# Loading w_q first, in eight 16-row pieces, and giving the last sums ten rows of w_out instead of six

## The chip, the cores and the metric

The kernel runs on one core of one Trainium2 chip. A core has five engines that run their own instruction streams and wait for each other through semaphores: PE (TensorE, matrix products; PEld is its loading of stationary operands), DVE (VectorE), ACT (ScalarE), POOL (GpSimd) and SP (SyncE, which here only issues DMAs). Sixteen DMA engines move data between HBM and the on-chip memory SBUF, which has 128 partitions; PE writes its results to a second memory, PSUM. The metric is the device time of one execution in microseconds (us), lower is better. The kernel before takes 128.52 us, the median of three runs (128.49 to 128.59).

## The reference, cut to what matters

One decoding step: one token, one row `x` of 576 numbers, layer-normed to `xn`. Two branches read `xn`, and the result is their sum with `x`.

```python
xn = layernorm(x)
# A: attention over the last 4096 positions of a cache, 32 query heads, 16 key heads, head size 128
q  = (xn @ wq)                      # wq: 576 x 4096
s  = q . k_cache[..., -4096:, :] * 128 ** -0.5
a  = softmax(s) . v_cache[..., -4096:, :]
A  = a.reshape(4096) @ wo           # wo: 4096 x 576
# B: a gated MLP
z  = gelu(xn @ w_in)                # w_in: 576 x 4608
g  = w_sp * layernorm(z[2304:]) + b_sp
B  = (z[:2304] * g) @ w_out         # w_out: 2304 x 576
out = x + A + B
```

Everything is bfloat16 in HBM. Keys and values are 16.8 MB each, w_q and w_o 4.7 MB each, w_in 5.3 MB and w_out 2.7 MB: 51 MB are read for very little arithmetic.

## The kernel before

The 16 key heads are worked on in four blocks of four heads (`b` = 0 to 3). A block's keys are one tile `kn[b]` of 128 partitions, with 32 KB in each; its values `vn[b]` likewise. w_q is one tile `wq_t` with 36,864 bytes in each partition (nine rows of 2048 numbers). Tiles come from two pools with two buffers each, `small` (32 KB per partition) and `large` (36 KB), so a load into a pool's third tile waits until the first one's readers are done. Two narrow leftovers, `win8` and `wo28`, share a third buffer.

The order of the work is the order of the program text: nothing is rearranged, and every engine runs its own part in that order. All large loads are issued by SP, and they are listed at the top of the kernel (lines 105 to 124) in the order in which the DMA engines then work them off: keys 0 in two halves, w_q in two pieces of five and four rows, keys 1, values 0, keys 2, values 1, keys 3, w_in, values 2, values 3, w_o, w_out in four pieces. ACT issues three tiny loads before (`x_row` and the two numbers `ws2`). Eight completion counters are used in turn by these loads, ACT's three included, so a load's issue also waits for the load eight places before it.

The compute side:

- `turn(b)` (line 214, DVE): eight transposes that turn the keys of a block into the eight tiles `kt`, which have eight buffers in all.
- the query: 36 products of w_q with `xn` into `q_ps` (line 225, PE), then a copy (229), a transpose (231), four products (234) and four multiplications into `zq` (238).
- `scores(b)` (line 261, PE): 32 products of `zq` with the `kt` tiles; then maximum, exponential and transpose on DVE and ACT (264 to 287).
- `values(b)` (line 295, PE) and its small followers (300 to 306).
- `gate(z_all())`: the products with w_in (line 319) and the gate, ending in `hv`, the 18 columns that meet w_out.
- the end: w_o and the first `LATE` = 12 rows of w_out (of FR = 18) are summed into two PSUM tiles `acc` as four partial rows each (line 390). These are copied to `acc_sb` (393 on ACT, 394 on DVE), the PSUM tile `fin` is set to zero (396), and `late` (line 400) adds into `fin` the remaining rows of w_out, four products per row, and the four partial rows of `acc_sb`, eight instructions. Then the result is rounded (409) and stored (410).

The calls stand in this order: `turn(0)`, the query, `scores(0)`, `turn(1)`, `scores(1)`, `values(0)`, `turn(2)`, `scores(2)`, `values(1)`, `turn(3)`, `scores(3)`, `gate(z_all())`, `values(2)`, `values(3)`, the end.

Of the kernel before, what the change touches and what calls it, by code (L numbers as in the profile page):

```python
# [8 lines left out]
FP32 = mybir.dt.float32  # L9
# [5 lines left out]
P = 128  # L15
D = 576
# [12 lines left out]
NR = 9  # L29
# [3 lines left out]
FR = FH // P  # L33
# [3 lines left out]
ZW = P + ZPAD  # L37
SMALL = NU * DH
LARGE = WR * D
LATE = 12  # L40
OW = D // 4


# [1 line left out]
def kernel(  # L45
# [14 lines left out]
    nc = tc.nc  # L60
# [11 lines left out]
    ps_v = ctx.enter_context(tc.tile_pool(name="ps_v", bufs=1, space=PS))  # L72
# [11 lines left out]
    def unit(name, width):  # L84
        pool = small if width == SMALL else large
        return pool.tile([P, width], BF16, name=name, tag="u")

    def halves(a):
        return a.rearrange("k (s c) -> (k s) c", s=2).rearrange("(p r) c -> p (r c)", r=NR)

    def load(t, view, width, cuts):
        for a, e in zip(cuts, cuts[1:]):
            nc.sync.dma_start(t[:, (a - cuts[0]) * width:(e - cuts[0]) * width], view[:, a * width:e * width])

    def load_kv(cache, name, b, width, cuts=(0, NU)):
        t = unit(f"{name}{b}", width)
        src = cache[0, HB * b:HB * (b + 1), SK - W:SK, :].rearrange("s (j u) d -> j s (u d)", u=NU)
        for a, e in zip(cuts, cuts[1:]):
            nc.sync.dma_start(t[:, a * DH:e * DH], src[:, :, a * DH:e * DH])  # L99
        return t  # L100

    kn, vn = {}, {}
    wq_v, win_v = halves(A_wq), halves(B_w_in)
    wo_v = A_wo.rearrange("(p r) n -> p (r n)", r=WR)
    kn[0] = load_kv(A_k_cache, "k", 0, SMALL, (0, NU // 2, NU))
    wq_t = unit("wq", LARGE)
    load(wq_t, wq_v, 2048, (0, 5, NR))
    kn[1] = load_kv(A_k_cache, "k", 1, SMALL)
    vn[0] = load_kv(A_v_cache, "v", 0, LARGE)
    kn[2] = load_kv(A_k_cache, "k", 2, SMALL)  # L110
# [10 lines left out]
    wo28 = one.tile([P, FH], BF16, name="wo28", tag="side")  # L121
    load(wo28, wo_v, D, (28, WR))
    wout_t = unit("wout", LARGE)
    load(wout_t, B_w_out.rearrange("(p r) n -> p (r n)", r=FR), D, (0, LATE, 16, 17, FR))


    ident = const.tile([P, P], BF16, name="ident")
# [83 lines left out]
    def turn(b):  # L211
        for k in range(NK):
            t = ktp.tile([P, 2, 512, 2], BF16, name=f"kt{b}_{k}", tag="kt")
            nc.vector.transpose(  # L214
                t[:].rearrange("p c n e -> p (c n e)").bitcast(FP32),
                kn[b][:, UK * DH * k:UK * DH * (k + 1)].bitcast(FP32).rearrange("p (u c i) -> p c u i", c=2, i=32))
            kt[b, k] = t

    turn(0)


    q_ps = ps_s.tile([P, 512], FP32, name="q_ps", tag="s")
# [30 lines left out]
    def scores(b):  # L253
        sm = one.tile([P, 2, 512], FP32, name=f"sm{b}", tag="sm")
        mx = work.tile([P, 2], FP32, name=f"mx{b}", tag="mx")
        for kk in range(2):
            s_ps = ps_s.tile([P, 512], FP32, name=f"s{b}_{kk}", tag="s")
            for k4 in range(4):
                for ce in range(4):
                    c, e = divmod(ce, 2)  # L260
                    nc.tensor.matmul(s_ps[:], lhsT=zq[:, b, ce, ZPAD - 8 * k4:ZPAD - 8 * k4 + P],  # L261
                                     rhs=kt[b, 4 * kk + k4][:, c, :, e],
                                     start=k4 == 0 and ce == 0, stop=k4 == 3 and ce == 3)
            nc.vector.tensor_tensor_reduce(  # L264
                out=sm[:, kk, :].rearrange("p (n s) -> p n s", s=HB),
                in0=s_ps[:].rearrange("p (n s) -> p n s", s=HB),
                in1=cm[:].unsqueeze(1).to_broadcast([P, P, HB]), scale=SCALE, scalar=-3e38,
                op0=ALU.add, op1=ALU.max, accum_out=mx[:, kk:kk + 1])
        m1 = work.tile([P, 1], FP32, name=f"m1{b}", tag="m1")
        nc.vector.tensor_max(m1[:], mx[:, 0:1], mx[:, 1:2])  # L270
        tr = ps_m.tile([P, P], FP32, name=f"tr{b}", tag="m")
        nc.tensor.matmul(tr[:], lhsT=m1[:].to_broadcast([P, P]), rhs=ident_f[:], start=True, stop=True)  # L272
        m8 = work.tile([P, 8], FP32, name=f"m8{b}", tag="m8")
        nc.vector.tensor_reduce(out=m8[:], in_=tr[:].rearrange("p (a x) -> p x a", x=8), axis=AXX, op=ALU.max)
        mj = work.tile([P, 8], FP32, name=f"mj{b}", tag="mj")
        nm = work.tile([P, 1], FP32, name=f"nm{b}", tag="nm")
        nc.vector.tensor_tensor_reduce(out=mj[:], in0=m8[:], in1=sel8[:], scale=-1.0, scalar=0.0,  # L277
                                       op0=ALU.mult, op1=ALU.add, accum_out=nm[:])
        p = one.tile([P, 1024], BF16, name=f"p{b}", tag="p")
        l = work.tile([P, 1], FP32, name=f"l{b}", tag="l")  # L280
        nc.scalar.activation(p[:], sm[:].rearrange("p k n -> p (k n)"), ACT.Exp, bias=nm[:], accum_out=l[:])  # L281
        p_t[b] = work.tile([P, 2, 16, 32], BF16, name=f"pt{b}", tag="pt")
        nc.vector.transpose(p_t[b][:].rearrange("p k u m -> p (k u m)"), p[:])  # L283
        su = ps_m.tile([P, 8], FP32, name=f"su{b}", tag="m")
        nc.tensor.matmul(su[:], lhsT=l[:].to_broadcast([P, P]), rhs=sel8[:], start=True, stop=True)  # L285
        rms[b] = work.tile([P, 8], FP32, name=f"rm{b}", tag="rm")
        nc.vector.reciprocal(rms[b][:], su[:])
# [39 lines left out]
    def gate(z):  # L327
# [26 lines left out]
                                op0=ALU.mult, op1=ALU.add)  # L354
        nc.vector.tensor_mul(hv[:], G[:, 0, :], gz[:])

    scores(0)
    turn(1)
    scores(1)
# [15 lines left out]
    o_p = const.tile([P, WR], BF16, name="o_p")  # L375
    nc.vector.tensor_copy(o_p[:], op_ps[:])

    acc = [ps_a.tile([P, HW], FP32, name=f"acc{i}", tag="a") for i in range(2)]
    for i in range(2):
        nc.vector.memset(acc[i][:], 0.0)  # L380
# [4 lines left out]
    rows += [(o_p[:, r:r + 1], wo28[:, D * (r - 28):D * (r - 27)]) for r in range(28, WR)]  # L385
    rows += [(hv[:, r:r + 1], wout_t[:, D * r:D * (r + 1)]) for r in range(LATE)]
    for n in range(0, len(rows), 4):
# [4 lines left out]
    acc_sb = const.tile([P, D], FP32, name="acc_sb")  # L392
    nc.scalar.copy(acc_sb[:, 0:HW], acc[0][:])
    nc.vector.tensor_copy(acc_sb[:, HW:D], acc[1][:])  # L394
    fin = ps_v.tile([P, OW], FP32, name="fin", tag="pv")
    nc.vector.memset(fin[:], 0.0)

    def late(col, w, n, start=False, stop=False):
        for g in range(4):
            nc.tensor.matmul(fin[32 * g:32 * g + 1, :], lhsT=col, rhs=w[:, n + OW * g:n + OW * (g + 1)],  # L400
                             start=start, stop=stop, tile_position=(0, 32 * g))

    for r in range(LATE, FR):
        if r == FR - 1:
            late(selu[:, 0:1], acc_sb, 0)
        late(hv[:, r:r + 1], wout_t, D * r, start=r == LATE, stop=r == FR - 1)

# [33 lines left out]
```

## Time and profile before

| | |
|---|---|
| median of three runs | 128.52 us |
| the profiled execution's own time | 129.87 us |
| its span, first to last instruction | 128.1 us |
| PE busy | 72.9 us (57%) |
| DVE busy | 65.3 us (51%) |
| ACT, POOL busy | 10.2 us, 3.9 us |
| HBM read | 50.96 MB, 398 GB/s over the span |
| DMA queue of SP, share of 16 engines | 93.4% |

The durations in the profile come from one execution, which took 129.87 us by its own clock and whose span is 128.1 us; 1.8 us lie around the span. The median of the unprofiled runs is 1% below that. Busy times of engines are totals over stages that have different limits; where time can be saved is read from the chain of waits and from the stretches in time, not from the totals. A line such as "L261 PE" names line 261 of the kernel.

### The profile page before, as it was taken

The numbers are of one execution on the slowest core, as the hardware profiler recorded it, in microseconds if no ns is written. First come the engines' busy times: TensorE is split into PE (matmuls) and PEld (weight loads), VectorE is DVE, ScalarE is ACT, GpSimd is POOL, SyncE is SP. The second block draws the span as 40 slices with busy tenths as digits, with TensorE's granted clock in tenths as the row PEclk, the third lists the DMA queues.
The fourth block names the chain that finished last, engine by engine and source line by source line (L and its number), as shares of the span: only waits on it lengthen the run. The fifth ranks groups of instructions, "written<-read, shape, count | busy, mean of one in ns | idle before, by whom it ended". The sixth has DMA issues, their size and how long they took to land.

```text
span 128.1 us, 1363 instructions
## 1 busy us (share of the span) xinstructions
PE 72.9 (57%) x554; PEld 33.7 (26%) x554; DVE 65.3 (51%) x133; ACT 10.2 (8%) x19; POOL 3.9 (3%) x10
## 2 busy tenths in 40 slices
PE   3200007349982399557599554899192389467070
PEld 3100002113421134123234233233080225323040
DVE  6689960060213999640899542998347620300010
ACT  3010000000003000031000031000300030100010
POOL 8400000000000000000000000000000000000000
PEclk9999999999999779986959999589977769855559
DMA  3999999998998999999989998999899899999810
GB/s 82 409 420 444 460 405 414 476 491 348 471 471 368 463 425 389 491 399 420 481 379 450 449 449 368 394 484 460 379 471 435 379 416 438 418 414 436 345 45 0
DMA packets 2899, 51.03 MB, mean 398 GB/s; under 512 B 333, under 2 KB 590, under 8 KB 974
## 3 DMA queue, kind: packets, MB, share of 16 engines
q1 hardware_dynamic: 2888, 50.96, 93.4%
q8 instruction: 4, 0.07, 0.2%
q14 instruction: 1, 0.01, 0.0%
q10 hardware_dynamic: 6, 0.00, 0.0%
HBM read 50.96 MB, written 0.00 MB: 398 GB/s over the span
## 4 chain that ended last, share of the span: by engine, by line
PE 37%; DMA 36%; DVE 16%; ACT 5%; SPq 2%; issue 1%; ACTq 0%
PE s L261 22%; DMA wout<-in_B_w_out_dram 19%; DMA wq<-in_A_wq_dram 17%; DVE kt L214 9%; PE pv L295 4%; ACT p L281 4%; PE z L319 3%; DVE sm L264 2%; PE op L303 2%; PE tr L272 2%; PE q_ps L225 2%; PE acc L390 1%; PE fin L400 1%; DVE pt L283 1%; SPq L99 1%
## 5 line engine op out<-in xcount | busy, mean ns | idle before, releaser
L261 PE MATMUL s<-kt,zq 128*128 128x512 bf16 x128 | 36.4, 448 | 5.3 <-DVE kt L214 4.9
L214 DVE STREAM_TRANSPOSE kt<-k 128x1024 f32<-128x1024 f32 x32 | 36.4, 1205 | 0.0
L261 PEld LDWEIGHTS <-zq 128*128 128x128 bf16 x128 | 14.0, 110 | 26.5 <-issue 15.3
L225 PE MATMUL q_ps<-wq,xw 128*32 128x512 bf16 x36 | 4.2, 626 | 16.4 <-DMA wq<-in_A_wq_dram 16.4
L264 DVE CUSTOM_DVE_ANT_1 sm<-s,cm 128x512 f32<-128x512 f32 x8 | 5.4, 677 | 10.1 <-PE s L261 10.1
L281 ACT ACTIVATE p<-sm,nm 128x1024 bf16<-128x1024 f32 x4 | 4.6, 1147 | 73.9 <-DVE nm L277 73.9
L295 PE MATMUL pv<-v,pt 128*32 128x512 bf16 x128 | 10.2, 477 | 0.0
L283 DVE STREAM_TRANSPOSE pt<-p 128x1024 bf16<-128x1024 bf16 x4 | 5.0, 1245 | 5.4 <-ACT p L281 5.4
L306 DVE TENSOR_TENSOR o_t<-op,rm 128x8 bf16<-128x8 f32 x4 | 0.7, 167 | 13.0 <-PE op L303 13.0
L225 PEld LDWEIGHTS <-xw 128*32 128x32 bf16 x36 | 1.4, 131 | 18.4 <-issue 18.4
L394 DVE COPY acc_sb<-acc 128x288 f32<-128x288 f32 x1 | 0.5, 458 | 11.2 <-PE acc L390 11.2
L285 PE MATMUL su<-sel,l 128*128 128x8 f32 x8 | 1.6, 266 | 7.6 <-ACT p L281 7.6
L303 PE MATMUL op<-selu,pvs 128*128 128x8 f32 x32 | 4.2, 259 | 2.8 <-ACT pvs L300 2.8
L390 PE MATMUL acc<-wo,o_p 128*1 128x288 bf16 x64 | 4.4, 439 | 1.7 <-DMA wo<-in_A_wo_dram 1.7
L303 PEld LDWEIGHTS op<-selu,pvs 128*128 128x128 f32 x32 | 3.9, 191 | 5.1 <-ACT pvs L300 5.1
L229 DVE CAST q_sb<-q_ps 128x512 bf16<-128x512 f32 x1 | 0.7, 692 | 8.2 <-PE q_ps L225 8.2
L295 PEld LDWEIGHTS <-pt 128*32 128x32 bf16 x128 | 3.6, 114 | 4.3 <-issue 2.6
L272 PE MATMUL tr<-ident_f,m 128*128 128x128 f32 x8 | 2.0, 326 | 3.9 <-DVE m L270 3.9
L319 PE MATMUL z<-win,xw 128*32 128x288 bf16 x72 | 3.6, 376 | 0.0
L285 PEld LDWEIGHTS su<-sel,l 128*128 128x128 f32 x8 | 1.2, 187 | 8.4 <-ACT p L281 8.4
L390 PE MATMUL acc<-wout,hv 128*1 128x288 bf16 x24 | 1.6, 438 | 3.0 <-DMA wout<-in_B_w_out_dram 3.0
L300 ACT COPY pvs<-pv 128x512 f32<-128x512 f32 x4 | 2.3, 586 | 11.0 <-PE pv L295 11.0
(95 smaller groups left out, 43.4 us busy)
## 6 DMA issues: line engine op xcount, KB each, us to landing
v<-in_A_v_cache_dram SPq DMA_DIRECT2D x4, 4096.0 KB, 25.8
k<-in_A_k_cache_dram SPq DMA_DIRECT2D x3, 4096.0 KB, 36.7
win<-in_B_w_in_dram SPq DMA_DIRECT2D x1, 4608.0 KB, 25.7
k<-in_A_k_cache_dram SPq DMA_DIRECT2D x2, 2048.0 KB, 9.8
wo<-in_A_wo_dram SPq DMA_DIRECT2D x2, 2016.0 KB, 27.1
wq<-in_A_wq_dram SPq DMA_DIRECT2D x1, 2560.0 KB, 17.4
wq<-in_A_wq_dram SPq DMA_DIRECT2D x1, 2048.0 KB, 21.6
wout<-in_B_w_out_dram SPq DMA_DIRECT2D x1, 1728.0 KB
```

The source lines that it names most:

```text
L214: nc.vector.transpose(t[:].rearrange("p c n e -> p (c n e)").bitcast(FP32), kn[b][:, UK * DH * k:UK * DH * (k + 1)].bitcast(FP32).rearrang ...
L225: nc.tensor.matmul(q_ps[32 * g:32 * g + 32, :], lhsT=xw[:, r, :], rhs=wq_t[:, 2048 * r + 512 * g:2048 * r + 512 * (g + 1)], start=r == 0, ...
L261: nc.tensor.matmul(s_ps[:], lhsT=zq[:, b, ce, ZPAD - 8 * k4:ZPAD - 8 * k4 + P], rhs=kt[b, 4 * kk + k4][:, c, :, e], start=k4 == 0 and ce = ...
L264: nc.vector.tensor_tensor_reduce(out=sm[:, kk, :].rearrange("p (n s) -> p n s", s=HB), in0=s_ps[:].rearrange("p (n s) -> p n s", s=HB), in ...
L272: nc.tensor.matmul(tr[:], lhsT=m1[:].to_broadcast([P, P]), rhs=ident_f[:], start=True, stop=True)
L281: nc.scalar.activation(p[:], sm[:].rearrange("p k n -> p (k n)"), ACT.Exp, bias=nm[:], accum_out=l[:])
L283: nc.vector.transpose(p_t[b][:].rearrange("p k u m -> p (k u m)"), p[:])
L285: nc.tensor.matmul(su[:], lhsT=l[:].to_broadcast([P, P]), rhs=sel8[:], start=True, stop=True)
L295: nc.tensor.matmul(pv[32 * g:32 * g + 32, :].rearrange("p (n d) -> p n d", n=4), lhsT=p_t[b][:, kk, u, :], rhs=v4[:, kk, u, :, :], start=k ...
L303: nc.tensor.matmul(op[:], lhsT=pvs[:, DH * u:DH * (u + 1)], rhs=selu[:, 8 * u:8 * u + 8], start=u == 0, stop=u == 3)
L319: nc.tensor.matmul(zp[i][32 * g:32 * g + 32, :], lhsT=xw[:, r, :], rhs=rhs, start=r == 0, stop=r == NR - 1, tile_position=(0, 32 * g))
L390: nc.tensor.matmul(acc[i][32 * g:32 * g + 1, :], lhsT=col, rhs=w[:, HW * i:HW * (i + 1)], start=n == 0 and g > 0, stop=n + 4 >= len(rows), ...
```

## The change

w_q moves ahead of keys 0. It is no longer cut by columns into two loads of 128 partitions, but by partitions into eight loads: load `e` fills the partitions e, e+8, e+16, ... e+120, which are 16 rows of 36,864 contiguous bytes each. `turn(0)` moves behind the query, directly ahead of `scores(0)`. At the end `LATE` is 8, so that ten rows of w_out go straight into `fin`; w_out comes in five pieces, which end at rows 8, 13, 16, 17 and 18; the zeroing of `fin` moves ahead of that of `acc`; and the partial rows of `acc_sb` are added ahead of row 13 instead of ahead of row 17.

```diff
-LATE = 12
+LATE = 8
...
+    wq_t = unit("wq", LARGE)
+    for e in range(8):
+        nc.sync.dma_start(wq_t[e::8, :], wq_v.rearrange("(i e) f -> e i f", e=8)[e])
     kn[0] = load_kv(A_k_cache, "k", 0, SMALL, (0, NU // 2, NU))
-    wq_t = unit("wq", LARGE)
-    load(wq_t, wq_v, 2048, (0, 5, NR))
     kn[1] = load_kv(A_k_cache, "k", 1, SMALL)
...
-    load(wout_t, B_w_out.rearrange("(p r) n -> p (r n)", r=FR), D, (0, LATE, 16, 17, FR))
+    load(wout_t, B_w_out.rearrange("(p r) n -> p (r n)", r=FR), D, (0, LATE, 13, 16, 17, FR))
...
-    turn(0)
...
+    turn(0)
     scores(0)
     turn(1)
...
+    fin = ps_v.tile([P, OW], FP32, name="fin", tag="pv")
+    nc.vector.memset(fin[:], 0.0)
     acc = [ps_a.tile([P, HW], FP32, name=f"acc{i}", tag="a") for i in range(2)]
...
     nc.vector.tensor_copy(acc_sb[:, HW:D], acc[1][:])
-    fin = ps_v.tile([P, OW], FP32, name="fin", tag="pv")
-    nc.vector.memset(fin[:], 0.0)
...
     for r in range(LATE, FR):
-        if r == FR - 1:
+        if r == 13:
             late(selu[:, 0:1], acc_sb, 0)
         late(hv[:, r:r + 1], wout_t, D * r, start=r == LATE, stop=r == FR - 1)
```

## The prediction

> **What bounds the kernel now.** I read the slices of the page first, then stretches of time, then the chain of waits, and last the timeline of the end.
>
> The page's slices: one column is 3.2 us.
>
> ```profile
> DMA  3999999998998999999989998999899899999810
> GB/s 82 409 420 444 460 405 414 476 491 348 471 471 368 463 425 389 491 399 420 481 379 450 449 449 368 394 484 460 379 471 435 379 416 438 418 414 436 345 45 0
> q1 hardware_dynamic: 2888, 50.96, 93.4%
> ```
>
> The DMA engines are busy from the first slice to the 38th. No engine of the core is (PE 57%, DVE 51%). Longer stretches of the same (PE, PEld, DVE, ACT, POOL busy, PE clock, DMA share, GB/s):
>
> ```profile
> 2.20:2.80 0.60, 0.60 (x7) 0.60 (x7) 0.60 (x1) 0.60 (x1) 0.60 (x1) 1.00 0.44 82
> 3.20:24.40 21.20, 3.10 (x24) 1.52 (x24) 13.12 (x29) 0.57 (x3) 1.33 (x3) 1.00 1.01 433
> 24.40:82.00 57.60, 40.94 (x213) 17.09 (x213) 32.98 (x58) 4.89 (x8) 0.00 (x0) 0.90 1.01 434
> 104.00:121.00 17.00, 10.26 (x131) 5.16 (x124) 1.35 (x7) 1.17 (x2) 0.00 (x0) 0.70 0.99 415
> 121.40:122.00 0.60, 0.48 (x12) 0.28 (x15) 0.00 (x0) 0.00 (x0) 0.00 (x0) 0.50 0.34 134
> ```
>
> From 3.2 to 82 us the rate is flat at 433 to 434 GB/s, 27.1 per DMA engine, whatever is loaded and computed. So 51 MB cost about 119 us, and only three things can move the time: when the stream starts, whether it keeps this rate, and what follows its end. Between 2.2 and 2.8 us its share is 0.44: about half of the engines have begun.
>
> The chain of waits, its end:
>
> ```profile
> 97.30 24.18 DMA wout<-in_B_w_out_dram
> 121.48 0.04 issue
> 121.52 1.64 PE acc L390 x24
> 123.16 0.02 issue
> 123.19 0.46 DVE acc_sb L394
> 123.64 0.03 issue
> 123.67 0.19 DVE fin L396
> 123.86 0.04 issue
> 123.90 1.33 PE fin L400 x26
> 125.23 0.02 issue
> 125.26 0.31 DVE res L409
> ```
>
> The first piece of w_out (rows 0 to 11) lands at 121.48. What ends the kernel then is not the last bytes but 3.75 us of PE and DVE work on that piece; rows 12 to 17 land beside it.
>
> **Part 1, the end of w_out.** A row is 147,456 B, 9.2 KB for each of 16 DMA engines, 0.34 us at 27.1 GB/s. Six rows follow the first piece, so the last lands at about 121.48 + 2.04 = 123.5. If the stream ended at the same moment, the new pieces would land at 120.1 (rows 0 to 7), 121.8 (8 to 12), 122.8 (13 to 15), 123.2 and 123.5. PE: 16 of the 24 products, 1.64 x 16/24 = 1.1, end at 121.2; the copies of `acc` (0.46) end at 121.7, hidden by the second piece. From 121.8, 20 products of `fin` (the timeline has 0.77 us for 20) to 122.6; the eight of `acc_sb` (0.6 from the first weight load to the next row's) to 123.2; rows 13 to 15, 12 products by the same rate 0.46, to 123.7; row 16 0.15; row 17 with its drain 0.26: 124.1. Before it was 125.23: **1.1 us less**. Bounds: 1.3 if the last landing decides (123.5 + 0.3), 0.7 if the products at half clock (0.50 there) overlap less. The zeroing of `fin` (0.18) leaves the chain; in its new place it delays the first `acc` product at 111.75, behind which PE idles 1.7 us for w_o, which hides it. One load more costs SP 0.43, issued some 20 us before its data move.
>
> **Part 2, w_q first.** The number of bytes ahead of keys 1 is the same, so nothing behind it lands later if the rate holds. At this rate w_q (4.72 MB) takes 10.9 us and lands at about 14.7 instead of 24.4. All its 36 products then run in one go (2.32 + 1.90 = 4.2), the query's small steps take 1.9 (26.36 to 28.28), so `turn(0)` could start at 20.8 instead of 9.0. It takes 9.1, ends at 29.9 instead of 18.1, and `scores(0)` about 1 us behind it: 31 instead of 37.8. `turn(0)` ending 12 us later delays the issue of keys 2, which wait for its buffer; they are then queued at 30 behind data that keep the engines busy to about 43 (17.3 MB), so nothing starves. `scores(1)` and all that follows start earlier, and then wait for loads: no gain at the end, because the chain already waits there for w_out.
>
> **Part 3, the form of the eight loads.** SP's issues take 0.53 to 0.65 each here; eight take at most 5.2, while each row of 36,864 B keeps an engine busy for 1.36. The start: with 16 rows instead of 128 to hand out, the late half of the engines can start with the first. That is worth between nothing and the 0.6 us of the half-empty stretch; I take 0.3, the middle, since nothing in the trace is nearer to either end.
>
> The rate of these loads is the large unknown. Every large load of before writes all 128 partitions at once, and the flat 433 belongs to that form. No row shows 16 rows on 16 partitions. If the limit of 27.1 lies in the DMA engines alone, w_q takes 10.9 us as w_in's rows of the same length do. If it lies in entrances of the memory that each serve a fixed group of partitions, 16 partitions that lie eight apart may share entrances two by two: each pair then takes turns, and w_q takes 21.8. [...] Below nothing the term cannot go, as 433 is the highest rate of any long stretch; above, four rows to an entrance would give 43.6. By its nearest row (w_in) it would be 10.9; I take the paired case, because a limit that is flat to 0.2% over 79 us, over loads of different lengths and sources, looks like a fixed width of a path, and a path's width is shared as soon as two writers meet in it. This is a judgement, not a reading: 0.5 against 0.35.
>
> [...]
>
> What a doubled w_q does behind it: it lands at about 25.6, keys 0 at 30.4 and 35.3 (4.85 a half). The query is done at 31.7, `turn(0)` at 40.9, `scores(0)` at about 42 instead of 37.8. That is 4.2 later, while every load behind is 10.9 later: the loads stay the bound, and all that waits for them moves by 10.9.
>
> **The sum.** +10.9 (w_q) - 1.1 (end) - 0.3 (start) = +9.5 us. The terms come from the profiled execution (129.87 us, span 128.1); the median of the runs, 128.52, is 1% below it, which changes differences of this size by 0.1. **128.5 + 9.5 = 138.0 us.**
>
> **The rivals.**
>
> *The loads run at the full rate, faster.* For it: w_in's 36,864 B rows take no longer per byte than others, the stream has no gap, and 16 rows give each DMA engine one row. Against it: the form has no row. The point from which it decides: each engine writing 27.1 GB/s into any partition. 128.5 - 1.1 - 0.3 = 127.1 us, chance 0.35.
>
> [...]
>
> *A new wait in SP.* The loads use eight completion counters in turn with ACT's three, so e = 5, 6 and 7 are issued only after the three tiny loads have landed, and everything else stands behind them. The engines hold seven rows by then, 9.5 us of work at full rate, to about 12. The tiny loads share DMA queues with rows of 1.36 us instead of 0.6. If they landed later than 12, the stream would stand still by the difference, and above 13.4 the gain of rival one would be gone. They are issued by 2 us, so this needs a delay of 10: chance 0.05, about 128.5.
>
> *The compute becomes the bound* in the slow case: it would need the chain to be more than 10.9 late, and it is 4.2: 0.01.
>
> **How the numbers follow.** Forecast (paired entrances) 0.50, half shared 0.09, full rate 0.35, the wait in SP 0.05, compute 0.01. I count 0.2% (0.26 us) as what can be told from no change. Slower: 0.50 + 0.09 + 0.01 + 0.02 of the wait in SP = 0.62. Faster: the full rate less a small share in which start and end give nothing, 0.34. Same: 0.04. The likeliest case's own range is 136.8 to 139.2 (start 0 to 0.6, end 0.7 to 1.3, w_q 21 to 23). The whole range must reach to the full-rate case, which holds more than 2 in 10: 126.5 to 139.2.
>
> **What would show it.** Paired: in the stretch from about 3 to 25 us the rate is near 217 GB/s, first `q_ps` product near 25 us, landings of keys, w_in and w_out all about 11 us later, rate back at 433 behind w_q. Full rate: 433 from 3 us on, first `q_ps` product near 14.7, `scores(0)` done at 31, first `acc` product with w_out near 120. The start: DMA share above 0.9 between 2.2 and 2.8. The end: `fin` products start ahead of the last landing, and the last `fin` product ends 0.6 us or less behind it. SP: a gap between e = 5 and keys 0 beyond 12 us would show the counters' wait. I am wrong if the 16-row loads keep the rate; then the end's 1.1 us are all that counts.

## The result and the profile after

The changed kernel takes 140.21 us (median, 140.10 to 140.32) against 128.59 us: the ratio is 1.0885, 95% interval 1.0848 to 1.0922, so 11.6 us slower. Forecast were 138.0 us, and a range that ended at 139.2. The direction and the slow form of the loads came out as forecast, the size did not: 9.5 us were announced and 11.6 measured.

The page of the changed kernel, its slices of 3.46 us (DMA share in tenths, then GB/s):

```profile
DMA  7899988899999999999999999998999999999950
GB/s 171 171 192 277 213 171 175 308 441 422 493 445 398 398 433 436 455 445 436 407 407 426 455 445 433 420 448 375 469 436 431 407 417 413 424 434 401 409 216 0
```

The DMA engines are as busy as before, but in the first seven slices they move half as much. Stretches of the same kernel (busy times of PE, PEld, DVE, ACT and POOL, PE clock, DMA share, GB/s):

```profile
3.20:24.40 21.20, 0.76 (x4) 0.61 (x3) 4.09 (x21) 0.55 (x3) 1.33 (x3) 1.00 0.95 196
35.00:92.00 57.00, 42.26 (x200) 18.19 (x199) 40.66 (x60) 4.89 (x8) 0.00 (x0) 0.78 1.01 434
```

From 3.2 to 24.4 us the rate is 196 GB/s where it was 433. Behind w_q it is 434 again. So the eight loads alone are slow, not what follows them. The timeline says when w_q had landed (the query waits for it), and when SP issues keys 2:

```profile
26.62 3.39 PE L224 MATMUL q_ps<-wq,xw 128*32 128x512 bf16 x36 [20.92 <-DMA wq<-in_A_wq_dram]
41.68 0.54 SPq L99 DMA_DIRECT2D k<-in_A_k_cache_dram  x1
```

The query starts at 26.62; w_q and both halves of keys 0, which before had landed by 24.4, are all there at 36.0 by the trace's landings, 11.6 later. The issue of keys 2, which waits for `turn(0)`, has moved to 41.7 and starves nothing (434 GB/s from 35 to 92 us). The end of the chain of waits:

```profile
84.20 33.45 DMA v<-in_A_v_cache_dram
117.66 0.02 issue
117.68 17.45 DMA wout<-in_B_w_out_dram
135.12 0.04 issue
135.16 0.26 PE fin L400 x4
135.43 0.02 issue
135.45 0.31 DVE res L409
```

The chain is now a DMA chain up to the last piece of w_out (135.12), and only four products and the rounding follow it. The new end works as described: 0.31 us from the last landing to the last product.

### The profile page after: what moved, and what is told of

It reads as the page before. It is cut to its first block, busy times and chain, and to the rows that moved or that the text cites. A ratio compares the mean times of both kernels' runs of the same rounds, so it can differ in the third digit from the quotient of the medians.

```text
span 138.3 us, 1388 instructions
## 1 busy us (share of the span) xinstructions
PE 76.2 (55%) x562; PEld 36.0 (26%) x562; DVE 65.2 (47%) x133; ACT 10.2 (7%) x19; POOL 3.9 (3%) x10
## 4 chain that ended last, share of the span: by engine, by line
DMA 55%; PE 30%; DVE 8%; ACT 3%; issue 1%; SPq 0%; ACTq 0%
DMA v<-in_A_v_cache_dram 24%; PE s L260 21%; DMA wq<-in_A_wq_dram 18%; DMA wout<-in_B_w_out_dram 13%; PE pv L294 3%; ACT p L280 3%; DVE kt L215 2%; PE q_ps L224 2%; DVE sm L263 2%; PE op L302 1%; PE tr L271 1%; DVE pt L282 1%; DVE m L273 1%; DVE zq L237 1%; PE su L284 1%
## 5 line engine op out<-in xcount | busy, mean ns | idle before, releaser
L260 PE MATMUL s<-kt,zq 128*128 128x512 bf16 x128 | 37.5, 461 | 6.9 <-DVE kt L215 6.9
L260 PEld LDWEIGHTS <-zq 128*128 128x128 bf16 x128 | 14.6, 114 | 28.7 <-issue 17.9
L224 PE MATMUL q_ps<-wq,xw 128*32 128x512 bf16 x36 | 3.4, 548 | 20.9 <-DMA wq<-in_A_wq_dram 20.9
L294 PE MATMUL pv<-v,pt 128*32 128x512 bf16 x128 | 11.8, 533 | 2.8 <-DMA v<-in_A_v_cache_dram 2.8
L302 PE MATMUL op<-selu,pvs 128*128 128x8 f32 x32 | 5.9, 311 | 2.7 <-ACT pvs L299 2.7
L302 PEld LDWEIGHTS op<-selu,pvs 128*128 128x128 f32 x32 | 5.5, 259 | 6.0 <-ACT pvs L299 6.0
L392 PE MATMUL acc<-wo,o_p 128*1 128x288 bf16 x64 | 3.7, 380 | 0.3 <-DMA wo<-in_A_wo_dram 0.3
L347 PE MATMUL sz_ps<-sz,ones_f 128*128 128x2 f32 x2 | 0.6, 365 | 4.6 <-DVE sz L344 4.6
```

Source lines behind the costliest of these rows:

```text
L224: nc.tensor.matmul(q_ps[32 * g:32 * g + 32, :], lhsT=xw[:, r, :], rhs=wq_t[:, 2048 * r + 512 * g:2048 * r + 512 * (g + 1)], start=r == 0, ...
L294: nc.tensor.matmul(pv[32 * g:32 * g + 32, :].rearrange("p (n d) -> p n d", n=4), lhsT=p_t[b][:, kk, u, :], rhs=v4[:, kk, u, :, :], start=k ...
L302: nc.tensor.matmul(op[:], lhsT=pvs[:, DH * u:DH * (u + 1)], rhs=selu[:, 8 * u:8 * u + 8], start=u == 0, stop=u == 3)
L392: nc.tensor.matmul(acc[i][32 * g:32 * g + 1, :], lhsT=col, rhs=w[:, HW * i:HW * (i + 1)], start=n == 0 and g > 0, stop=n + 4 >= len(rows), ...
```

## The experiments

**One load instead of eight.** Everything else of the changed kernel stays.

```diff
-    for e in range(8):
-        nc.sync.dma_start(wq_t[e::8, :], wq_v.rearrange("(i e) f -> e i f", e=8)[e])
+    nc.sync.dma_start(wq_t[:], wq_v)
```

> The changed kernel with w_q in one load of 128 partitions instead of eight of 16; its place ahead of the keys, turn(0) behind the query and the new end stay. Theory A (entrances: a load of 128 partitions reaches every entrance of the memory, one of 16 partitions eight apart reaches half of them): the first 25 us run at 433 GB/s again, the first product of the query at about 14.7 us, and the time is 128.6 - 1.1 to 1.3 (the end) = 127.3 to 127.5 us. Theory B (place: w_q ahead of the keys is what costs): stays near 140. Theory C (36,864 B rows, or their distance in HBM, are slow as the first load): the rate of the first 25 us stays below 300 GB/s and the time is 132 to 140.

Measured: 128.36 us, ratio to before 0.9961 (0.9934 to 0.9987). The query starts at 14.5 us. Its stretches:

```profile
3.20:24.40 21.20, 7.04 (x50) 3.39 (x51) 9.70 (x32) 0.50 (x2) 1.33 (x3) 0.93 0.99 424
24.40:82.00 57.60, 42.35 (x201) 18.50 (x203) 40.99 (x60) 4.89 (x8) 0.00 (x0) 0.79 1.01 433
```

The loss is in the form of the loads, not in their place or in the length of the rows. But 127.3 to 127.5 were expected for the rest of the change; about 1 us of the gain is missing.

**The distance of the rows in HBM.** The eight loads read neighbouring rows of w_q instead of rows 294,912 B apart, into the same partitions.

```diff
-        nc.sync.dma_start(wq_t[e::8, :], wq_v.rearrange("(i e) f -> e i f", e=8)[e])
+        nc.sync.dma_start(wq_t[e::8, :], wq_v[16 * e:16 * e + 16, :])
```

> The changed kernel, but load e reads 16 neighbouring rows of w_q in HBM into the partitions e, e+8, ... e+120. w_q's rows so lie in the wrong partitions, so the query is another one; bytes, loads and partitions written are the same. Theory A (the shared thing lies on the side of the on-chip memory): no change, 140.2 within 0.3, a row of 36,864 B still takes about 2.9 us. Theory C (the distance of 294,912 B between the rows that are read at the same time in HBM): 433 GB/s from the start and 127.3 to 128.5.

Measured: 140.02 us, 196 GB/s from 3.2 to 24.4 as in the changed kernel:

```profile
3.20:24.40 21.20, 0.76 (x4) 0.60 (x3) 4.09 (x21) 0.56 (x3) 1.33 (x3) 1.00 0.95 196
```

What is shared does not lie on HBM's side, as far as the distance of the rows goes.

**Sixteen neighbouring partitions.**

```diff
-        nc.sync.dma_start(wq_t[e::8, :], wq_v.rearrange("(i e) f -> e i f", e=8)[e])
+        nc.sync.dma_start(wq_t[16 * e:16 * e + 16, :], wq_v[16 * e:16 * e + 16, :])
```

> The changed kernel, but each of the eight loads fills 16 neighbouring partitions (16e to 16e+15) instead of every eighth; the query stays right. [...] Theory A2 (any 16 partitions share in pairs, or 16 rows in a load run at half rate for another reason, such as the count of rows or loads): 140.2. Theory A3 (neighbours do not collide): 127 to 129.

Measured: 157.54 us, ratio 1.2256 (1.2214 to 1.2298); the query starts at 44.2. Its stretches:

```profile
13.00:24.00 11.00, 0.00 (x0) 0.00 (x0) 0.00 (x0) 0.00 (x0) 0.00 (x0) 1.00 0.94 107
46.00:110.00 64.00, 45.60 (x226) 19.23 (x218) 43.85 (x68) 4.89 (x8) 0.00 (x0) 0.79 1.01 434
```

Number, size and source of the loads are those of the run before this; only the partitions differ, and the rate is about a quarter of 433. So the partitions decide. The trace has a record for every row that a DMA engine moved: a row of 36,864 B takes 5.12 us here, 2.87 in the changed kernel and 1.36 in the run with one load. The author's estimate of 162 to 164 us was missed because a row here takes 3.75 times as long as alone, not 4 to 4.2 times, and the first sixteen only 4.2 us.

**Fewer and larger loads:** four loads of 32 rows (every fourth partition), and two of 64 (every second).

```diff
-    for e in range(8):
-        nc.sync.dma_start(wq_t[e::8, :], wq_v.rearrange("(i e) f -> e i f", e=8)[e])
+    for e in range(4):
+        nc.sync.dma_start(wq_t[e::4, :], wq_v.rearrange("(i e) f -> e i f", e=4)[e])
```

For two loads of 64 rows, each 4 in these lines is a 2.

> The changed kernel with w_q in four loads of 32 rows, every fourth partition. [...] Theory B (loads with fewer than 128 rows are slow by their number of rows): half of the loss, about 134.

> The changed kernel with w_q in two loads of 64 rows, every second partition. [...] Theory B (by the number of rows): about 131.

Measured: 128.84 us (ratio 0.9976 to 1.0037) and 128.77 us (0.9955 to 1.0028). The stretch of the run with 32 rows:

```profile
3.20:13.00 9.80, 0.77 (x4) 0.60 (x3) 4.09 (x21) 0.50 (x3) 1.33 (x3) 1.00 0.98 421
```

Both run at nearly the full rate (421 GB/s, and 425 with 64 rows, from 3.2 to 13 us), and a row takes 1.36 to 1.38 us behind the first turn (a turn is one row for each of the 16 DMA engines). So a small number of rows does not halve the rate. On the reading of entrances, the engines here write at different ones at the same time; that is a conclusion from the rate, no record names an entrance. The two versions are 0.4 to 0.5 us slower than the one load (128.36); part of that is the start, as their first rows begin at 2.1 us and those of the one load at 1.75.

**Eight rows at a time.** Sixteen loads of 8 rows, eight partitions apart, first in the lower and then in the upper half of the partitions.

```diff
-    for e in range(8):
-        nc.sync.dma_start(wq_t[e::8, :], wq_v.rearrange("(i e) f -> e i f", e=8)[e])
+    for h in range(2):
+        for e in range(8):
+            nc.sync.dma_start(wq_t[64 * h + e:64 * h + 64:8, :],
+                              wq_v[64 * h:64 * h + 64, :].rearrange("(i e) f -> e i f", e=8)[e])
```

> The changed kernel with w_q in sixteen loads of 8 rows, eight partitions apart, of the lower half of the partitions (e, e+8, ... e+56) and then of the upper half. Only eight DMA engines work. [...] Rival (those 64 apart share, the lower half's do not): a row takes 1.37 us, sixteen 22 us, the time 138.5 to 140.5.

Measured: 169.46 us, ratio 1.3138 (1.3043 to 1.3233). The stretches, DMA share and GB/s in the last two columns:

```profile
2.20:24.00 21.80, 1.76 (x12) 1.52 (x11) 5.09 (x21) 1.61 (x3) 2.33 (x3) 1.00 0.51 108
28.00:50.00 22.00, 0.00 (x0) 0.00 (x0) 0.00 (x0) 0.00 (x0) 0.00 (x0) 1.00 0.98 145
```

With a share of 0.51, half of the DMA engines work, and still their rows take 2.87 us each: a row is as slow as with sixteen rows spread over both halves, so on the reading of pairs these lie within a half and are not those 64 apart. From 28.6 us SP issues keys 0 and the other eight DMA engines begin with it: the share goes to 0.98. A row of w_q then takes 3.7 to 4.1 us, and by the same records a 16 KB row of keys 0 takes 1.83 us, where it takes 0.61 in the kernel before. So each of the sixteen engines is down to about a third of its rate, more than pairs alone would cost. This had not been expected: w_q is complete at 54.3 us, where 16 rows of 2.87 would have ended near 48, and so the author's estimate from such rows, 163 us, was missed. Where the sixteen meet, no run here tells.

**The new end alone**, in the kernel before (the lines of the diff in the section on the change that speak of `LATE`, the cuts of w_out, `fin` and `r == 13`):

```diff
-LATE = 12
+LATE = 8
```

> The kernel before with the new end alone (ten rows of w_out in the last sums, five pieces, zeroing moved). Theory A: the end costs 0.3 us behind the last landing instead of 1.6, so 127.2 to 127.5 us. Rival: the profiled execution of before took 129.87 us where its median is 128.59, so its end was not that of the usual execution; then the usual gain is 0 to 0.5 and the time is 128.1 to 128.6.

Measured: 128.69 us, ratio 0.9994 (0.9965 to 1.0024). The rival holds: no gain, although the new end does sit close behind the last landing, at 123.61:

```profile
106.18 17.43 DMA wout<-in_B_w_out_dram
123.65 0.26 PE fin L400 x4
```

**The old end in the changed kernel**, the same lines undone:

> The changed kernel with the old end put back (six rows in the last sums); the eight loads and turn(0) as changed. Theory A, terms that add up: 140.2 + 1.3 = 141.5 us. Rival (the end is worth less in usual executions): 140.2 to 140.7.

Measured: 141.38 us, 1.2 more than with the new end. Here the end is worth what was forecast. The two runs contradict each other unless the end depends on something else, and TensorE's granted clock (third figure from the end of a stretch's line) says on what. The stretch with the last products in the run with the old end:

```profile
134.00:137.00 3.00, 1.61 (x37) 0.83 (x32) 0.94 (x3) 0.40 (x1) 0.00 (x0) 0.50 0.05 16
```

TensorE has half its clock there. With the new end alone it was 1.00 from 121.5 to 124.

**A second profile of the kernel before.**

> The kernel before, unchanged, for a second profile. The first profiled execution took 129.87 us, the median is 128.59. Theory: the end differs by TensorE's clock: where it is granted 1.0 instead of 0.5 behind 121 us, the 24 products of the last sums take about 0.9 instead of 1.64 us and the last products about 0.9 instead of 1.33, the span is 126.8 and the last product of fin ends within 0.5 us of the last landing, as in the kernel with the new end alone. Rival: the difference lies in the loads (the last landing 1.3 us earlier). If the profile again takes 129.9 us nothing is told apart.

Measured: a median of 128.59 us, and a span of 126.7 where the first profile had 128.1. Its stretch, and the end of its chain:

```profile
121.50:124.00 2.50, 1.51 (x56) 0.89 (x48) 0.80 (x3) 0.40 (x1) 0.00 (x0) 1.00 0.16 57
```

```profile
98.47 22.80 DMA wout<-in_B_w_out_dram
121.27 0.04 issue
121.31 0.94 PE acc L390 x24
122.25 0.02 issue
122.27 0.46 DVE acc_sb L394
122.72 0.03 issue
122.75 0.19 DVE fin L396
122.94 0.04 issue
122.99 0.82 PE fin L400 x32
123.81 0.02 issue
```

At clock 1.00 the same steps of the same kernel take 0.94 instead of 1.64 and 0.82 instead of 1.33 us, and the last product ends at 123.81. The last row of w_out landed at 123.47 by the trace's landings, so 0.34 us before that: the old end already sat where the new end can reach. Of the 60 executions of the kernel before that were timed beside the experiments, 10 took 129.7 to 130.1 us; the profile that the forecast was made from, with 129.87, was of this kind.

**One load ahead of the keys, old end** (the place alone; `turn(0)` stands behind the query as in the change):

```diff
     kn, vn = {}, {}
...
+    wq_t = unit("wq", LARGE)
+    nc.sync.dma_start(wq_t[:], wq_v)
     kn[0] = load_kv(A_k_cache, "k", 0, SMALL, (0, NU // 2, NU))
-    wq_t = unit("wq", LARGE)
-    load(wq_t, wq_v, 2048, (0, 5, NR))
```

> The kernel before with w_q in one load ahead of the keys and turn(0) behind the query; the old end. Theory: the place alone is worth the earlier start of the stream, 0.2 to 0.4, and the new end nothing where TensorE has its full clock at the end, so 128.2 to 128.5 us; with half the clock at the end 129.4 to 129.8, which the new end would have saved.

Measured: 129.65 us, ratio 1.0067 (1.0043 to 1.0091), the second of the two outcomes expected. Its end:

```profile
121.57 1.61 PE L389 MATMUL acc<-wout,hv 128*1 128x288 bf16 x24 [4.12 <-DMA wout<-in_B_w_out_dram]
```

With w_q ahead, the compute is done with w_o early, TensorE idles 4.12 us before the last sums (in the second profile of before 1.69), and the sums run at the half clock (0.50 from 121.3 to 125): 1.61 us. All twelve executions took 129.4 to 130.1. With the new end the half clock is there too (0.50 from 121 to 124), but it costs nothing, which is the 128.36 of the first experiment.

**The eight loads alone**, at w_q's old place behind keys 0, with the old order and end:

> The kernel before with one part alone: w_q in the eight loads of 16 rows, at its old place behind keys 0; turn(0) and the end as before. Theory A (the form costs, wherever it stands): w_q's rows take 2.88 instead of 1.37 us, +11.8, so 140.2 to 141.6 us (the upper end if TensorE has half its clock at the end). Theory B (the form costs only at the start of the stream): below 133.

Measured: 141.78 us (three executions at 141.6 to 142.1, one at 140.16), ratio 1.0953 (1.0872 to 1.1034). The form costs nearly the same wherever it stands: a row takes 2.82 us here and 2.87 with w_q ahead. The time is a little above the expected 140.2 to 141.6, and not through the clock alone, as the timeline of this run shows:

```profile
130.78 4.01 PE L391 MATMUL acc<-wo,o_p 128*1 128x288 bf16 x64
134.58 1.04 PE L391 MATMUL acc<-wout,hv 128*1 128x288 bf16 x24
```

The products with w_out follow those with w_o without a wait for a load. With the query not starting before 36.2 us, the compute has become the bound at the end; the last row of w_out lands at 134.9, and the last product ends 2.3 us later. TensorE had half its clock from 131 to 134 us while it was busy throughout, so the clock has a part in this; how large a part was not separated.

## Why the prediction was right and wrong

*The stream bounds the kernel; only its start, its rate and what follows its end matter: right.* Everything behind w_q landed 11.5 to 11.6 us later, at an unchanged rate, and the compute stayed covered (`turn(0)` ended at 41.7, forecast 40.9).

*The paired entrances: half the rate came as forecast, the size did not.* The runs on HBM distance and neighbours, which differ in the partitions alone, show that the partitions a load fills decide its rate (196 against 107 GB/s). The runs with 32 rows (421 GB/s) and with eight (a row in 2.87 us) fit pairs of partitions that take turns. In rates, 16 rows of 36,864 B in 2.87 and in 5.12 us are 205 and 115 GB/s. That entrances are what is shared remains the author's reading, and which partitions make a pair no run here tells. The size was w_q = twice 10.9. In the trace a row takes 2.87 us, not 2 x 1.37 = 2.74 (in the kernel before, the same bytes come in two pieces of 0.76 and 0.61 us); eight of them, less 0.2 in the fifth turn (below), are 22.8 us instead of 11.0: **+11.8 where the sum had +10.9**. The prediction's own bounds for w_q, 21 to 23, held this, but its range was added up wrongly: with 23 for w_q, 0.7 for the end and 0 for the start the likeliest case reaches 128.5 + 12.1 - 0.7 = 139.9, not 139.2. The measured 140.2 lies above both. The rival at the full rate is out by the 196 GB/s. So is the one with the chance of 0.09, half shared, in which one engine of a pair is served first: the 16 engines' rows begin and end within 1.6 us of each other in every turn, so no engine of a pair runs ahead.

*The end, -1.1: wrong, and this is the larger error.* The step that failed is in the sum: "The terms come from the profiled execution (129.87 us, span 128.1); the median of the runs, 128.52, is 1% below it, which changes differences of this size by 0.1". That 1% was not spread over the execution. Beside the second profile the last product of `fin` ended 1.42 us later (125.23 against 123.81), of which 0.21 were there when the first piece of w_out landed (121.48 against 121.27); the other 1.2 lay in the PE work behind it, on which the change acts, because in that execution TensorE was at half its clock there. Measured against the usual execution the end is worth nothing (ratio 0.9994); in the two kernels with w_q ahead, whose old end ran at the half clock, it is worth 1.2 to 1.3 us (141.38 against 140.21, and 129.65 against 128.36). The prediction had shown the half clock (0.50 from 121.4 to 122.0) and named it as a bound of the gain, but as a property of the kernel. So -1.1 was taken off a median that did not have these 1.2 us in it.

*The start, -0.3: about right.* 11.8 for w_q against 11.6 for everything behind leaves -0.2; this is a remainder, no run measured the term alone. The reason given is seen in the records: before, eight DMA engines begin their first row at 2.2 us and the other eight at 2.8 to 3.0; in the changed kernel all 16 begin between 2.1 and 2.7.

*SP's counters: no effect*, as forecast, though the working was off. Of the eight issues only the seventh waited noticeably, 2.1 us, and it waited for the first load of w_q, which landed at 6.64 us. So SP had issued six loads by then, not the five that the prediction's own count gives, nor the seven that it took. The tiny loads, which have a queue of their own on the profile's page (q10) and share none with the rows, had landed by 6.9 us. The eight issues were out by 7.8 us, while the DMA engines had rows until beyond 20.

The sum with what was measured: +11.8 + 0 - 0.2 = +11.6, which is the difference of the medians (the -0.2 being what closes it). One more figure of the prediction does not come out, though nothing rests on it: 51 MB at 433 GB/s are 118 us, not 119.

## What to carry to other kernels

A load that keeps all DMA engines busy can still run at half or a quarter of the rate: look at GB/s beside the DMA share, and choose the partitions of a load with care (every fourth or every second partition ran at 421 and 425 GB/s here, every eighth at 196 and sixteen neighbours at 107). Before a gain is worked out from a profile, compare the profiled execution's own time with the median; if it lies 1% above, find where that 1% sits, and if it sits in the step that the change removes, the gain may be there in some executions only. An end that waits for the last load instead of for products is no faster here than the old end at full clock (128.69 us, ratio 0.9994), but half the clock no longer hurts it: the version with one load of w_q ahead of the keys and the new end took 128.36 us against 128.59 for the kernel before (ratio 0.9961, 0.9934 to 0.9987), and none of its twelve executions took more than 128.8.

## What the runs showed of the hardware that was not expected

A row of 36,864 B takes 1.364 us alone, 2.87 with every eighth partition and 5.12 with sixteen neighbours. The second is 5% more than twice the first, the third 6% less than four times it. Why was not settled, nor why beside keys 0 sixteen engines were each down to a third (3.7 to 4.1 us for such a row).

In w_q's fifth turn a row takes 2.68 us instead of 2.87; the same dip is seen in the run with the loads at their old place (2.59 against 2.82). No run shows its cause.

The times of the kernel before gather near 128.5 and near 129.8 us, with a few near 129.0, and its two profiles, one near 128.5 and one near 129.8, differ by TensorE's clock in the last 3 us. What makes the clock fall stays open. Over all thirteen profiles, TensorE idled 2.2 to 4.1 us before its first product with w_out in seven, and all seven have half the clock in the last sums. It idled 1.6 to 1.7 us in four; three of these fall to half the clock before the last products, and one, the second profile of the kernel before, does not. In two it did not idle, and they end at full clock. So longer idling goes with the half clock, but it is not shown to be the cause: in the first profile of the kernel before the clock is 0.50 all the way from 115 to 121.5 us, and TensorE idles only from 118.5.
